# A conditional block's transfers moved from SyncE's queue to GpSimd's queue

## Chip, cores and metric

The kernel runs on one core of one Trainium2 chip. The metric is the device time of one execution in microseconds (us), lower is better.

Three things are compared in time: the median of several executions, the span of the one profiled execution (first to last instruction), and what I call the **tail**: the end of the span minus the start of VectorE's last instruction, the add that completes the last output tile. The tail is there because the whole run scatters by some 3 us, while the end of the program repeats to a few tenths.

## The reference

Two branches are added to the input. Branch A is a recurrent attention: 64 segments of 32 tokens, each with 8 memory rows that are the previous segment's output. Branch B is a mixer and an MLP. Cut:

```python
def _A_ref(x, mem0, Wq, Wk, Wv, Wo, seg_len):
    mem = mem0
    for s in range(n_seg):                      # 64 segments, serial
        h = jnp.concatenate([mem, xs], axis=1)  # 8 + 32 rows
        q, k, v = ...                           # einsum with Wq, Wk, Wv (1024 x 32 heads x 128)
        p = _softmax(masked scores)
        o = ...                                 # p @ v, then Wo
        mem = o[:, :M, :]
        outs.append(o[:, M:, :])
...
xn = _layernorm(x, axis=-1)
return x + _A_ref(xn, ...) + _B_ref(xn, ...)
```

## The kernel before

The main program doesn't walk the segments one after the other. It estimates all memory rows ahead, computes all segments in parallel, and counts at the end how many memory rows miss a tolerance. Only if that count is above zero does a conditional block compute everything again, serially. Matmuls, stores and the check at the end of the main program, then the block (cuts are marked):

```python
# class Out: one output tile; its residual load and its store
if hg == (6 if self.late else 0):
    self.Rt = iop.tile([P, 512], F32, tag="Rt")
    nc.gpsimd.dma_start(self.Rt[:, :self.w], R_v[:, self.gi, self.cc])              # L723
...
nc.vector.tensor_tensor(ot[:, :self.w], self.ps[:, :self.w], self.Rt[:, :self.w], op=ALU.add)   # L731
(self.queue or nc.gpsimd).dma_start(out_v[:, self.gi, self.cc], ot[:, :self.w])     # L732
...
for o, q in zip(rest[-3:], (nc.sync, nc.sync, nc.scalar)):   # queues of the last three stores
    o.queue = q
...
nc.vector.tensor_scalar(cnt[:], nok[:], -1.0, float(NQ - 1), op0=ALU.mult, op1=ALU.add)
nc.vector.tensor_tensor(cnt[:], psc[:1, :1], cnt[:], op=ALU.add)
nc.vector.tensor_copy(flag_i[:], cnt[:])
for o in rest[2:]:
    for p in range(8):
        o.piece(p)

cond = nc.values_load(flag_i[0:1, 0:1], min_val=0, max_val=NQ + P)                  # L890
with tc.If(cond > 0):                                                               # L891
    ...
    nc.sync.dma_start(wo_sb[:], Wo_v)
    nc.sync.dma_start(mask40[:], mask40_d.ap())
    ...
    with tc.For_i(0, NSEG, 1) as i:                                                 # L911, 64 turns
        nc.sync.dma_start(xs[:], xn_d[bass.ds(i * SEG, SEG), :])
        nc.sync.dma_start(Rt[M:L, :], R_d[bass.ds(i * SEG, SEG), :])
        ...
        for hg in range(8):
            wq = fw.tile([P, KT, 512], BF16, tag="w")
            nc.sync.dma_start(wq[:], Wq_v[:, :, cs_])
            ...                                     # wk and wv the same: 24 loads of 1 MB a turn
        ...
        nc.sync.dma_start(out[0][bass.ds(i * SEG, SEG), :], ot[M:L, :])
```

## Time and profile before

| what | before |
|---|---|
| median time (3 executions) | 1516.68 us (1515.07 to 1517.8) |
| span of the profiled execution | 1512.7 us |
| TensorE busy | 1502.8 us, 99% |
| VectorE, ScalarE, GpSimd busy | 36%, 33%, 12% |
| start of VectorE's last add | 1508.87 us |
| tail (1512.7 - 1508.87) | 3.8 us |

The page of the kernel before: its span, busy time by engine, the moved data by DMA queue (q1, called hardware_dynamic, has SyncE's transfers; q0, software_dynamic, has GpSimd's), and the engines on the chain that ended last.

```profile
span 1512.7 us, 24295 instructions
...
PE 1502.8 (99%) x9778; PEld 807.9 (53%) x9850; DVE 545.2 (36%) x1138; ACT 504.1 (33%) x1142; POOL 178.9 (12%) x248
...
q1 hardware_dynamic: 281248, 189.92, 50.5%
q0 software_dynamic: 22032, 82.54, 15.8%
...
PE 98%; DMA 1%; issue 0%; ACT 0%; DVE 0%; SPq 0%
```

TensorE is busy all the time and is nearly the whole chain, so queues matter only where TensorE waits for a transfer, and after TensorE's last matmul.

Does the conditional block run? Asking the trace of before for a tile that only the block uses gives this:

```profile
nothing on hseg; most used: ['ps', 'wt', 'w_sb', 'hTb', 'oX', 'xT', 'h3T', 'QT', 'wo_sb', 'V', 'pso', 'psO', 'xn3T', 'psS', 'sm', 'PT', 'KT', 'xn2T', 'hTB', 'wot', 'oT_m', 'sums', 'Pn', 'rs', 'MZ']
```

So it doesn't. What is left of the block is the branch over it. The instructions of the kernel before at the line of the `If` (L891); columns: engine, operation, count, shortest/median/longest duration in ns, start of the first and of the last in us. A `q` after the engine's name means its sequencer.

```profile
L891 SPq EVENT_SEMAPHORE  x8: 17/17/17, 1506.8 to 1511.0; - x8
L891 POOLq COMPARE_BRANCH  x1: 54/54/54, 1503.4 to 1503.4; - x1
L891 SPq COMPARE_BRANCH  x1: 58/58/58, 1506.2 to 1506.2; - x1
L891 PEldq COMPARE_BRANCH  x1: 3495/3495/3495, 1507.3 to 1507.3; - x1
```

The reader should see two things. SyncE runs eight semaphore instructions (a semaphore is a counter that engines wait on and advance). I read them so: the skipped block would have advanced eight counters of transfers, so the path around the block waits for each and advances it by hand. And TensorE's branch takes 3.5 us where the others take under 0.1 us.

After the branch comes the program's closing code (all on L1015, the line that closes the program). In the kernel before, in the same columns: SyncE's list of waits (from 1511.0 us), GpSimd's four steps of the closing barrier, and SyncE's three drains, of which the first, at 1511.8 us, ends its list of waits. The second fence is the same view for GpSimd alone, 1495 to 1511 us, which singles out its first drain:

```profile
L1015 SPq EVENT_SEMAPHORE  x14: 17/28/28, 1511.0 to 1512.6; - x14
L1015 POOLq EVENT_SEMAPHORE  x4: 17/17/17, 1511.9 to 1512.6; - x4
...
L1015 SPq DRAIN  x3: 7/7/13, 1511.8 to 1512.1; - x3
```

```profile
L1015 POOLq DRAIN  x1: 5785/5785/5785, 1503.6 to 1503.6; - x1
```

GpSimd has a drain of 5.785 us, which starts at 1503.6 and is over at 1509.4 us. SyncE works through a list of waits and reaches its own closing drain at 1511.8 us. The closing barrier follows (from 1511.9 us). The end of the work itself, from the timeline of before (start, duration, engine, line, operation):

```profile
1502.87 0.54 POOL L723 DMA_DIRECT2D Rt<-R_scratch  x1 [5.65 <-DVE ot L731]
...
1508.87 0.42 DVE L731 TENSOR_TENSOR ot<-pso,Rt 128x256 bf16<-128x256 f32 x1 [3.07 <-PE pso L725]
1509.33 0.38 ACTq L732 DMA_DIRECT2D out_dram<-ot  x1
```

### The profile page before, as it was taken

To read this page: it belongs to the slowest core of one execution; us is meant where nothing else is said; L and a number is where in the kernel's file an instruction comes from. 1 tells how busy PE (TensorE), PEld (TensorE's weight loads), DVE (VectorE), ACT (ScalarE), POOL (GpSimd) and SP (SyncE) were. 2 spreads that over 40 slices of the span, in tenths; PEclk is the share of its full clock that TensorE was granted. 3 is DMA by queue.
4 is the path that set the end of the run, shared out by engine and by line. 5 is a ranking of instruction groups with operands and counts; after the bars stand their busy time and mean duration, and the time that the engine had idled before them with its cause. 6 is when DMAs were issued, how large, how long until landed. Compare 5 with 4: busy or idle time off the path is not lost.

```text
span 1512.7 us, 24295 instructions
## 1 busy us (share of the span) xinstructions
PE 1502.8 (99%) x9778; PEld 807.9 (53%) x9850; DVE 545.2 (36%) x1138; ACT 504.1 (33%) x1142; POOL 178.9 (12%) x248
## 2 busy tenths in 40 slices
PE   9999999999999999999999999999999999999998
PEld 7844444445444444444466645664665455545555
DVE  8382230100020122222246624651564166516642
ACT  6533203013012011111256614650663266416630
POOL 5231020211111231100000010001000100010001
PEclk9999999999999999999999999999999999999999
DMA  8699762353345887632399947992998299818811
GB/s 295 147 255 334 218 176 91 137 202 112 125 163 145 196 274 253 208 120 84 126 245 242 246 124 183 245 238 71 239 248 203 73 227 224 216 60 212 190 47 52
DMA packets 303539, 274.11 MB, mean 181 GB/s; under 512 B 153926, under 2 KB 270184, under 8 KB 303424
## 3 DMA queue, kind: packets, MB, share of 16 engines
q1 hardware_dynamic: 281248, 189.92, 50.5%
q0 software_dynamic: 22032, 82.54, 15.8%
q8 instruction: 79, 1.29, 0.4%
q14 instruction: 36, 0.29, 0.1%
q10 hardware_dynamic: 144, 0.07, 0.0%
HBM read 190.93 MB, written 46.14 MB: 157 GB/s over the span
## 4 chain that ended last, share of the span: by engine, by line
PE 98%; DMA 1%; issue 0%; ACT 0%; DVE 0%; SPq 0%
PE ps L667 30%; PE pso L725 15%; PE ps L595 15%; PE ps L537 13%; PE ps L563 13%; PE ps L395 4%; PE ps L318 3%; PE psS L682 2%; PE psO L706 2%; PE ps L860 1%; PE ps L487 1%; PE gps L466 0%; PE ps L452 0%; DMA PT<-Pn 0%; DMA xt<-in_A_x_dram 0%
## 5 line engine op out<-in xcount | busy, mean ns | idle before, releaser
L667 PE MATMUL ps<-hTb,wt 128*128 128x396 bf16 (+2 forms) x2528 | 497.5, 343 | 0.0
L667 PEld LDWEIGHTS <-wt 128*128 128x128 bf16 x2528 | 232.8, 98 | 166.4
L595 PE MATMUL ps<-wt,xT 128*128 128x512 bf16 x1003 | 220.1, 379 | 1.1
L725 PE MATMUL pso<-wo_sb,oX 128*128 128x512 bf16 (+1 forms) x972 | 209.3, 372 | 1.1
L537 PE MATMUL ps<-xn3T,w_sb 128*128 128x512 bf16 x896 | 196.2, 379 | 0.0
L563 PE MATMUL ps<-w_sb,h3T 128*128 128x512 bf16 x873 | 194.3, 379 | 1.2
L595 PEld LDWEIGHTS <-xT 128*128 128x128 bf16 x1024 | 100.2, 98 | 120.8
L538 ACT ACTIVATE h3T<-ps 128x512 bf16<-128x512 f32 x112 | 66.8, 597 | 290.4 <-PE ps L537 289.5
L725 PEld LDWEIGHTS <-oX 128*128 128x128 bf16 x992 | 96.1, 98 | 106.5
L673 ACT CAST KT<-ps 128x462 bf16<-128x462 f32 (+2 forms) x160 | 81.9, 512 | 191.0 <-PE ps L667 189.2
L563 PEld LDWEIGHTS <-h3T 128*128 128x128 bf16 x896 | 87.0, 98 | 103.3
L537 PEld LDWEIGHTS <-w_sb 128*128 128x128 bf16 x896 | 86.6, 98 | 102.1
L688 DVE TENSOR_REDUCE sums<-sm 99x4 f32<-99x396 f32 (+2 forms) x176 | 97.6, 555 | 113.2 <-ACT sm L686 113.2
L675 ACT ACTIVATE QT<-ps 128x462 bf16<-128x462 f32 (+2 forms) x160 | 83.9, 525 | 113.1 <-PE ps L667 101.5
L597 ACT CAST Vs<-ps 128x512 bf16<-128x512 f32 x64 | 37.5, 586 | 233.2 <-PE ps L595 174.9
L684 DVE TENSOR_TENSOR sm<-psS,c_mask_reg_sb 99x396 f32<-99x396 f32 x152 | 86.7, 570 | 76.9 <-PE psS L682 76.9
L686 ACT ACTIVATE sm<-sm 99x396 f32<-99x396 f32 (+2 forms) x176 | 92.7, 527 | 59.0 <-DVE sm L684 54.1
L601 DVE CAST Vs<-ps 128x512 bf16<-128x512 f32 x64 | 44.3, 692 | 170.0 <-PE ps L595 160.4
L694 DVE TENSOR_TENSOR Pn<-sm,rs 99x396 bf16<-99x396 f32 (+2 forms) x176 | 98.9, 562 | 7.3 <-DMA PT<-Pn 1.2
L564 DVE TENSOR_TENSOR R<-ps,R 128x512 f32<-128x512 f32 x32 | 21.9, 690 | 180.5 <-PE ps L563 166.3
L732 POOL DMA_DIRECT2D out_dram<-ot x30 | 16.3, 545 | 587.2 <-DVE ot L731 581.4
L731 DVE TENSOR_TENSOR ot<-pso,Rt 128x512 bf16<-128x512 f32 (+1 forms) x33 | 22.3, 675 | 171.7 <-PE pso L725 166.3
(124 smaller groups left out, 1071.5 us busy)
## 6 DMA issues: line engine op xcount, KB each, us to landing
wt<-in_A_Wq_dram SPq DMA_DIRECT2D x76, 512.0 KB
wt<-in_A_Wk_dram SPq DMA_DIRECT2D x76, 512.0 KB
wt<-in_A_Wv_dram POOLq DMA_DIRECT2D x24, 1024.0 KB, 6.6
V_scratch<-Vs SPq DMA_DIRECT2D x32, 512.0 KB
V<-V_scratch SPq DMA_DIRECT2D x40, 384.0 KB
R_scratch<-x POOLq DMA_DIRECT2D x16, 512.0 KB, 5.1
R<-R_scratch SPq DMA_DIRECT2D x16, 512.0 KB
R_scratch<-R POOLq DMA_DIRECT2D x16, 512.0 KB, 3.6
```

Of the source, the lines that this page charges most:

```text
L537: nc.tensor.matmul(ps[:].rearrange("p (n t) -> p n t", t=P), w3_sb[:, k, f * P:(f + 1) * P], xn3T[tb][:, :, k, :], start=(k == 0), stop=(k ...
L538: nc.scalar.activation(h3T[:, f, :], ps[:], ACTF.Gelu_apprx_tanh)
L563: nc.tensor.matmul(ps[:], h3T[:, f, j * P:(j + 1) * P], w4_sb[:, f, ch * 512:(ch + 1) * 512], start=(f == 0), stop=(f == FT - 1))
L595: nc.tensor.matmul(ps[:], xT[:, m4 * 4 + j, k, :], wv[:, k, :], start=(k == 0), stop=(k == KT - 1))
L667: nc.tensor.matmul(ps[:, :nb] if flat else ps[:, :nb].rearrange("p (t c) -> p t c", t=nt), w[:, k, hh * P:(hh + 1) * P], B["rhs"](k), star ...
L673: nc.scalar.copy(o, i)
L675: nc.scalar.mul(o, i, scale)
L684: nc.vector.tensor_tensor(sm[:T, :, :T], S3, t["mask"][:].unsqueeze(1).to_broadcast((T, 4, T)), op=ALU.add)
L686: nc.scalar.activation(e[:T, :, :T], sm[:T, :, :T], ACTF.Exp, scale=LN2)
L688: nc.vector.tensor_reduce(ss, e[:T, :, :T], axis=AX.X, op=ALU.add)
L694: nc.vector.tensor_tensor(Pn[:T, :, :T], e[:T, :, :T], rs[:T, :].unsqueeze(2).to_broadcast((T, 4, T)), op=ALU.mult)
L725: nc.tensor.matmul(self.ps[:, :self.w], self.oX[0][:, h, self.oX[1] + self.gl * P:self.oX[1] + (self.gl + 1) * P], wo_sb[:, h, self.cc], s ...
```

## The change

The intent is to take the block's transfers off SyncE's queue. Eight issue sites change, all inside the block:

```diff
-            nc.sync.dma_start(wo_sb[:], Wo_v)
+            nc.gpsimd.dma_start(wo_sb[:], Wo_v)
...
-            nc.sync.dma_start(mask40[:], mask40_d.ap())
+            nc.gpsimd.dma_start(mask40[:], mask40_d.ap())
...
-                nc.sync.dma_start(xs[:], xn_d[bass.ds(i * SEG, SEG), :])
-                nc.sync.dma_start(Rt[M:L, :], R_d[bass.ds(i * SEG, SEG), :])
+                nc.gpsimd.dma_start(xs[:], xn_d[bass.ds(i * SEG, SEG), :])
+                nc.gpsimd.dma_start(Rt[M:L, :], R_d[bass.ds(i * SEG, SEG), :])
...
-                    nc.sync.dma_start(wq[:], Wq_v[:, :, cs_])
+                    nc.gpsimd.dma_start(wq[:], Wq_v[:, :, cs_])
...   (wk, wv the same)
-                nc.sync.dma_start(out[0][bass.ds(i * SEG, SEG), :], ot[M:L, :])
+                nc.gpsimd.dma_start(out[0][bass.ds(i * SEG, SEG), :], ot[M:L, :])
```

More of the change, by code (lines that the diff above doesn't have):

```diff
@@ L921 @@
                     wq = fw.tile([P, KT, 512], BF16, tag="w")
-                    nc.sync.dma_start(wq[:], Wq_v[:, :, cs_])
+                    nc.gpsimd.dma_start(wq[:], Wq_v[:, :, cs_])
                     wk = fw.tile([P, KT, 512], BF16, tag="w")
-                    nc.sync.dma_start(wk[:], Wk_v[:, :, cs_])
+                    nc.gpsimd.dma_start(wk[:], Wk_v[:, :, cs_])
                     wv = fw.tile([P, KT, 512], BF16, tag="w")
-                    nc.sync.dma_start(wv[:], Wv_v[:, :, cs_])
+                    nc.gpsimd.dma_start(wv[:], Wv_v[:, :, cs_])
                     ps = fps.tile([P, 4, L], F32, tag="mm")
```

## The prediction

> **What bounds the kernel now.** TensorE. The table of busy time gives PE 1502.8 us of a 1512.7 us span (99%), at full granted clock in every slice; the chain of waits is 98% PE. DMA is 1% of that chain.
>
> **What the change touches.** Eight DMA issue sites, all inside the conditional block after the main program (the serial recomputation, taken only if a check count is above zero). Evidence that this run doesn't take it:
> - Asking the trace for tiles that exist only there (`hseg`, `mask40`, `QTa`, `oTs`, `mb`) gives nothing.
> - By line, the count is loaded once per engine (476 to 596 ns), each engine has one compare-and-branch, and after the last output store comes only the closing barrier, to 1512.6 us.
> - If it ran, each of 64 turns would load 24 weight tiles of 1 MB, 1.6 GB in all; at the 181 GB/s this run averages that is over 8 ms (my estimate). The whole run is 1.5 ms and moves 274 MB.
>
> So the change removes, adds and moves no executed transfer. The inputs are fixed and the arithmetic of the count is untouched, so the branch goes the same way.
>
> **What may still move.** Code placed around the block:
> 1. Bookkeeping on the path that skips the block. SyncE now runs eight semaphore instructions of 17 ns at the branch's line (1506.8 to 1511.0 us, waiting for its stores), because the skipped block would have advanced SyncE's DMA counters. This should leave SyncE and appear on GpSimd. SyncE saves at most about 0.1 us (8 x 17 ns); GpSimd branches at 1503.4 us and then sits in a drain of 5.8 us, so some 5 us of bookkeeping there is free.
> 2. Branch distance. The branch takes 54 ns on GpSimd and ScalarE, 58 on SyncE, 72 on VectorE, but 3495 ns on TensorE, over the longest skipped body. (The Trainium skill, "Advanced Engine Details and Errata", Control Flow Timing, gives about 108 ns for a compare-and-branch; four engines are below it, TensorE far above.) GpSimd's skipped body grows to about SyncE's of now, jumped in 58 ns, so I expect the same; even at 3.5 us it would end near 1507 us, ahead of TensorE's branch (1507.3 + 3.5 = 1510.8 us), which with ScalarE's last store (issued at 1509.3 us) sets the end.
> 3. The main program's order is fixed before the block; I expect identical instruction groups.
>
> The Trainium skill, "DMA: Bandwidth & Descriptors", Issuing engines are not separate DMA queues, says that transfers from any queue run on the same 16 engines. That would matter if the block ran; no run here shows it.
>
> **Prediction.** Change from structure: -0.2 to +0.5 us. The spread before is 1515.07 to 1517.8 us. So 1516.5 us, 8 in 10 within 1512.5 to 1520.5 us. Faster by over 2%: 1.5%; within 2%: 97%; slower by over 2%: 1.5%.
>
> **What would show it.** Right: PE busy 1503 us, the same groups and counts, the same MB per queue (q1 189.9, q0 82.5), still nothing on `hseg`, semaphore instructions at the branch's line gone from SyncE and present on GpSimd, and an instruction count within some 20 of 24295. Wrong on point 2: GpSimd's branch in the microseconds. Wrong altogether: MB moving between queues, a changed order of DVE or ACT groups, or a tail after 1509 us longer by more than 1 us.
>
> **What would make it wrong.** The build letting the block influence scheduling, semaphore assignment or memory layout of the main program; GpSimd's bookkeeping taking over 5 us; or GpSimd-issued transfers in a loop needing setup at the program's start.

## The result and the profile after

Ratios here are the mean time of one kernel's fast runs over that of the other's fast runs of the same rounds, so not quite the ratio of the medians quoted.

| what | before | after |
|---|---|---|
| median time (6 executions each) | 1515.14 us (1514.63 to 1517.8) | 1516.55 us (1516.22 to 1517.49) |
| ratio, 95% interval | | 1.0007 (0.9994 to 1.0019): the same |
| span | 1512.7 us | 1514.8 us |
| start of VectorE's last add | 1508.87 us | 1509.44 us |
| tail | 3.8 us | 5.4 us |

By its time the change does nothing that these runs can tell from zero, as predicted. The page after, the lines that answer to those of before:

```profile
span 1514.8 us, 24364 instructions
...
PE 1506.2 (99%) x9850; PEld 807.6 (53%) x9850; DVE 545.1 (36%) x1138; ACT 504.3 (33%) x1142; POOL 179.6 (12%) x248
...
q1 hardware_dynamic: 281248, 189.92, 50.3%
q0 software_dynamic: 22032, 82.54, 15.9%
...
PE 98%; DMA 1%; ACT 0%; DVE 0%; SPq 0%; issue 0%
```

The bytes and packets in each queue are the same to the last digit, and the trace again has nothing on `hseg`. The 3.4 us more of TensorE busy time is records: after has 9850 matmul records, before 9778, and some are missing from a trace now and then (both have 9850 weight loads). In the two traces the working instructions ahead of the branch are the same, in the same order, on every engine (9850 weight loads, 1138 instructions of VectorE, 1142 of ScalarE, 160 transfers of GpSimd, 630 of SyncE); only the incomplete matmul records can't be compared one by one. VectorE's last add starts 0.57 us later, which is within the scatter of the main program.

The end, however, is 1.5 us longer (5.36 against 3.83 us of tail). Around the branch and in the closing code of after, the same views as above:

```profile
L891 POOLq EVENT_SEMAPHORE  x4: 17/42/43, 1504.5 to 1506.4; - x4
L891 POOLq COMPARE_BRANCH  x1: 54/54/54, 1504.0 to 1504.0; - x1
L891 POOLq INC_SWDGE_SEM  x1: 1591/1591/1591, 1506.5 to 1506.5; - x1
L891 SPq COMPARE_BRANCH  x1: 58/58/58, 1506.8 to 1506.8; - x1
L891 PEldq COMPARE_BRANCH  x1: 3435/3435/3435, 1507.9 to 1507.9; - x1
```

```profile
L1015 SPq EVENT_SEMAPHORE  x14: 17/28/1615, 1508.1 to 1514.7; - x14
L1015 POOLq EVENT_SEMAPHORE  x4: 17/17/17, 1514.0 to 1514.7; - x4
...
L1015 SPq DRAIN  x3: 7/7/7, 1511.6 to 1514.2; - x3
```

```profile
L1015 POOLq DRAIN  x1: 5785/5785/5785, 1508.2 to 1508.2; - x1
```

```profile
1503.44 0.54 POOL L723 DMA_DIRECT2D Rt<-R_scratch  x1 [5.65 <-DVE ot L731]
...
1509.44 0.42 DVE L731 TENSOR_TENSOR ot<-pso,Rt 128x256 bf16<-128x256 f32 x1 [3.07 <-PE pso L725]
1509.89 0.38 ACTq L732 DMA_DIRECT2D out_dram<-ot  x1
```

The bookkeeping moved as expected: SyncE's eight semaphore instructions are gone, and GpSimd has four that wait and one that advances its counters (INC_SWDGE_SEM, 1.591 us). The waits end at 1506.4 us; the last transfer they can be waiting for is GpSimd's residual load issued at 1503.44 us. The counter update follows. Only then, at 1508.2 us instead of 1503.6, does GpSimd start its closing drain, and that drain takes exactly the same 5.785 us. It ends at 1514.0 us, and at 1514.0 us the closing barrier begins. SyncE was ready at 1511.6 us. So GpSimd is now the last to arrive.

That gives **theory A**: GpSimd's closing drain is work of a fixed length, not a wait for others, so everything put ahead of it moves its end; the 4.2 us between branch and drain (0.2 before) used up the slack and 1.5 us more. Its rivals: **B**, the end waits for GpSimd's counters through SyncE, and the drain only waits for the rest; **C**, the longer tail is scatter or comes from the code placed behind the branch.

### The profile page after: what moved, and what is told of

The parts are those of the page before. It is cut to its first block, busy times and chain, and to the rows that moved or that the text cites. A ratio compares the mean times of both kernels' runs of the same rounds, so it can differ in the third digit from the quotient of the medians.

```text
span 1514.8 us, 24364 instructions
## 1 busy us (share of the span) xinstructions
PE 1506.2 (99%) x9850; PEld 807.6 (53%) x9850; DVE 545.1 (36%) x1138; ACT 504.3 (33%) x1142; POOL 179.6 (12%) x248
## 4 chain that ended last, share of the span: by engine, by line
PE 98%; DMA 1%; ACT 0%; DVE 0%; SPq 0%; issue 0%
PE ps L667 30%; PE pso L725 15%; PE ps L595 15%; PE ps L537 13%; PE ps L563 13%; PE ps L395 4%; PE ps L318 3%; PE psS L682 2%; PE psO L706 2%; PE ps L860 1%; PE ps L487 1%; PE ps L452 0%; PE gps L466 0%; DMA PT<-Pn 0%; DMA xt<-in_A_x_dram 0%; PE ps L308 0%
```

## The experiments

All runs returned correct results.

### e1: the block's transfers on ScalarE's queue

```diff
-  nc.sync.dma_start(...)      # the eight sites of the block
+  nc.scalar.dma_start(...)
```

> The kernel before, with the fallback's transfers on ScalarE's queue in place of SyncE's: moved off SyncE, but not to GpSimd. Tail = end of the span minus the start of VectorE's last add (3.8 us before, 5.4 us after the change). Theory A (GpSimd's closing drain takes a fixed 5.8 us from wherever it starts, and the skip path's bookkeeping on GpSimd delayed its start from 1503.6 to 1508.2 us): no bookkeeping on GpSimd, the drain starts about 0.2 us after GpSimd's branch, the tail is 3.8 us within 0.3; the eight counter instructions are on ScalarE. Theory C (the longer tail is scatter between executions or follows from leaving SyncE): the tail is 5.4 us, or anywhere between. Time against before: 0.999 to 1.001 under each.

Median 1515.58 us (4 executions) against 1515.64 for before in the same rounds; ratio 0.9992 (0.9962 to 1.0022). The tail is 1513.7 - 1509.84 = 3.9 us. GpSimd's drain in e1, and the semaphore instructions at the branch's line:

```profile
L1015 POOLq DRAIN  x1: 5785/5785/5785, 1504.6 to 1504.6; - x1
```

```profile
L891 SPq EVENT_SEMAPHORE  x8: 17/17/17, 1507.4 to 1512.0; - x8
```

A detail of the expectation was wrong: the eight counter instructions stay on SyncE, though the block's transfers are ScalarE's. The point holds: with nothing owed on GpSimd, the drain starts 0.2 us after GpSimd's branch (at 1504.4 us) and the tail is that of before. It is not leaving SyncE's queue that costs; it is using GpSimd's. (Since the eight stay on SyncE, e1 doesn't show what SyncE gains by losing them; e3, e11 and e12 do.)

### e2: one site out of eight

```diff
-            nc.sync.dma_start(mask40[:], mask40_d.ap())
+            nc.gpsimd.dma_start(mask40[:], mask40_d.ap())
```

> The kernel before, with only the fallback's mask load (one of the eight sites) moved to GpSimd's queue, so that one counter of GpSimd's is owed on the skip path, not eight. Theory A: a counter update on GpSimd at the branch's line, with at most one wait; if the 1.59 us of the update goes with the number of counters it is well under 0.5 us here, the drain starts before 1505 us and the tail is 3.8 us within 0.3. If the update's cost is fixed, it is about 1.6 us, the drain starts near 1505.3 and ends near 1511.1, and the tail is 3.8 to 4.2 us. Theory B (SyncE's closing waits for GpSimd's counters set the end): 3.8 us as well.

One execution, 1515.73 us, tail 1513.5 - 1509.68 = 3.8 us.

```profile
L891 POOLq INC_SWDGE_SEM  x1: 1565/1565/1565, 1504.4 to 1504.4; - x1
```

```profile
L1015 POOLq DRAIN  x1: 5785/5785/5785, 1506.0 to 1506.0; - x1
```

The second of the two guesses came true: the update is hardly cheaper for one counter (1.565 us) than with all eight sites moved (1.591 us). A single transfer of 26 KB in a block that never runs buys the whole update. But with one counter there is no wait for the last residual load, so the drain starts at 1506.0 us and is over (1511.8 us) before SyncE arrives (1512.6 us). No longer tail.

### e3: the change, and GpSimd at its branch earlier

```diff
-                    nc.gpsimd.dma_start(self.Rt[:, :self.w], R_v[:, self.gi, self.cc])
+                    (nc.scalar if self.queue else nc.gpsimd).dma_start(self.Rt[:, :self.w], R_v[:, self.gi, self.cc])
```

This is applied to the kernel after; it moves the last three residual loads to ScalarE.

> The kernel after, with the last three residual loads (256 KB, 128 KB, 128 KB; the last GpSimd transfers before the branch) issued from ScalarE. The skip path's bookkeeping on GpSimd stays. Theory A: GpSimd reaches its branch some 5 us earlier, near 1498 us, the update takes the same 1.6 us, the drain of 5.8 us ends before 1508 us and no longer ends last: tail 3.8 us within 0.4, so the change's 1.5 us is gone though all that the change added is still there. Theory C (more code behind GpSimd's branch, or the update itself, lengthens the end): tail stays near 5.4 us.

Median 1514.53 us (4 executions), ratio to before 0.9985 (0.9955 to 1.0015). Tail 1512.8 - 1509.46 = 3.3 us.

```profile
L891 POOLq COMPARE_BRANCH  x1: 54/54/54, 1497.5 to 1497.5; - x1
L891 POOLq INC_SWDGE_SEM  x1: 1531/1531/1531, 1499.1 to 1499.1; - x1
```

```profile
L1015 POOLq DRAIN  x1: 5540/5540/5540, 1500.6 to 1500.6; - x1
```

All that the change added is still executed (four waits, an update of 1.531 us, a drain of 5.540 us), but GpSimd's branch comes 6.5 us earlier and the drain is over at 1506.1 us. The extra 1.5 us is gone. That is against C. The tail is even below the stated band (3.8 within 0.4); e11 and e12 take that up.

### e4: no change in the block, but GpSimd held up otherwise

```diff
-        for o, q in zip(rest[-3:], (nc.sync, nc.sync, nc.scalar)):
+        for o, q in zip(rest[-3:], (nc.sync, nc.sync, nc.gpsimd)):
```

This is applied to the kernel before.

> The kernel before (fallback on SyncE, no bookkeeping on GpSimd), with the very last output store issued from GpSimd's queue in place of ScalarE's. Theory A: GpSimd's drain can start only after its branch, near 0.5 + 0.5 + 0.3 us after that store's start, takes 5.8 us again and ends last: tail 7.5 to 8.5 us, span and time about 4 to 5 us (0.3%) longer than before. Theory B (SyncE's wait for the counters sets the end; the drain is only a wait for the others): tail 3.8 to 4.8 us.

Median 1519.93 us (4 executions, 1518.92 to 1520.22) against 1515.64, ratio 1.0021 (0.9991 to 1.0051; one execution of before, at 1523.43 us, widens it). Tail 1516.9 - 1508.70 = 8.2 us.

```profile
L1015 POOLq DRAIN  x1: 5867/5867/5867, 1510.1 to 1510.1; - x1
```

The block is that of before and no counter is owed on GpSimd. Still, with one store of 64 KB on GpSimd after the last add, the drain starts at 1510.1 us, takes 5.867 us and ends at 1516.0 us; SyncE was at its closing drain at 1511.8 us. The tail grows by 4.4 us, as A said and B did not. Here, as in after, the barrier begins where the drain ends. (The path of B exists: in after SyncE's first closing wait is met at 1508.1 us, when GpSimd's counter update ends. But SyncE is through its list at 1511.6 us, 2.4 us before the barrier.)

### e5: the kernel after again

No edit.

> The kernel after again, unchanged: how far do its tail (5.4 us) and GpSimd's bookkeeping (update 1.59 us, drain 5.785 us) repeat? Theory A: tail 5.4 us within 0.3, drain 5.78 us within 0.05. Time against before: theory A says about +1.5 us, a ratio of 1.001. If the tail comes back near 3.8 us, theory A falls.

Median 1516.3 us (5 executions) against 1515.46 (9), ratio 1.0012 (0.9999 to 1.0026). Tail 1514.3 - 1509.06 = 5.2 us; the update took 1.591 and the drain 5.785 us again, to the nanosecond. The longer tail is no scatter.

### e6: ten transfers fewer on GpSimd's queue

```diff
-                    (self.queue or nc.gpsimd).dma_start(out_v[:, self.gi, self.cc], ot[:, :self.w])
+                    if self.queue is None:
+                        stores[0] += 1
+                    q = self.queue or (nc.scalar if stores[0] > 20 else nc.gpsimd)
+                    q.dma_start(out_v[:, self.gi, self.cc], ot[:, :self.w])
```

This is applied to the kernel after (with `stores = [0]` set up earlier); the four lines shift the program's closing line from L1015 to L1019 and the branch from L891 to L895. GpSimd issues 150 transfers in the main program rather than 160 (counted in the traces).

> The kernel after, with the last ten output stores that GpSimd issued now issued by ScalarE; GpSimd's last residual loads stay, so its branch comes at the same place. What the drain's 5.8 us is made of: with 157, 160 and 161 transfers on GpSimd's queue it took 5.540, 5.785 and 5.867 us, 0.082 us for each one more. If it works off a list of GpSimd's transfers, ten fewer give 4.97 us within 0.1 and a tail of about 4.5 us (0.8 us less than after); if it is a fixed time, 5.8 us and 5.4 us.

One execution, 1515.26 us, tail 1513.7 - 1509.46 = 4.2 us.

```profile
L895 POOLq INC_SWDGE_SEM  x1: 1391/1391/1391, 1506.5 to 1506.5; - x1
```

```profile
L1019 POOLq DRAIN  x1: 4968/4968/4968, 1507.9 to 1507.9; - x1
```

The drain is 4.968 us; 4.97 was expected. The tail is 1.1 us shorter than that of after rather than 0.8, mostly because the update became shorter too, by 0.200 us (0.020 us a transfer). The drain's length is not a constant: from 150 to 161 transfers it goes with how many GpSimd has issued. e7 and e8 show that this number alone doesn't fix it.

### e7: 63 transfers fewer

```diff
-                    nc.gpsimd.dma_start(self.Rt[:, :self.w], R_v[:, self.gi, self.cc])
+                    nc.scalar.dma_start(self.Rt[:, :self.w], R_v[:, self.gi, self.cc])
...
-                    (self.queue or nc.gpsimd).dma_start(out_v[:, self.gi, self.cc], ot[:, :self.w])
+                    (self.queue or nc.scalar).dma_start(out_v[:, self.gi, self.cc], ot[:, :self.w])
```

This is applied to the kernel after.

> The kernel after, with all 63 residual loads and output stores of the attention part moved from GpSimd's to ScalarE's queue (97 transfers stay on GpSimd's). List theory: drain of 5.785 - 63 x 0.082 = 0.6 us, or another length that is far from 5.8 us if the list is shortened in between; the counter update shorter too. Fixed time: 5.8 us. Either way GpSimd is at its branch before 1500 us, so the tail is 3.3 to 3.9 us.

One execution, 1515.42 us, tail 1513.8 - 1510.72 = 3.1 us.

```profile
L891 POOLq INC_SWDGE_SEM  x1: 711/711/711, 1499.6 to 1499.6; - x1
```

```profile
L1015 POOLq DRAIN  x1: 2192/2192/2192, 1500.3 to 1500.3; - x1
```

The straight line (0.6 us) is a miss, and 5.8 us is a miss as well. At 0.082 us each, the drain's loss of 3.593 us is 44 transfers, not 63; at 0.020 us each, the update's loss of 0.880 us is 44 as well. Two different instructions that agree on 44 speak for one common list of transfers, of which some entries leave before the end. By the same reckoning (my estimate from these steps) the list of after has some 71 entries at the end, 5.785 / 0.0817, though 160 transfers were issued. Which ones leave, and when, no run here shows. The tail, 3.1 us, is a little under the stated 3.3 to 3.9.

### e8: no block at all

```diff
-    cond = nc.values_load(flag_i[0:1, 0:1], min_val=0, max_val=NQ + P)
-    with tc.If(cond > 0):
-        ... (the whole block)
```

This is applied to the kernel before. It gives up the guard, so it is a measurement and no candidate.

> The kernel before with the whole conditional block taken out (the count is still made, nothing reads it): what does the guard cost when it is not taken? TensorE's branch of 3.5 us and the register loads leave; the end is then the last store's landing or GpSimd's drain (5.8 us from about 1503 us, so done by 1509.5 us). Tail 3.0 to 3.7 us, at most 0.8 us less than before; time within 0.1% of before. If the tail falls by more than 1 us, the branch and not the store set the end of before.

Median 1514.13 us (4 executions), ratio 0.9989 (0.9974 to 1.0005). Tail 1512.3 - 1509.26 = 3.0 us. So a guard that isn't taken costs about 0.8 us of tail before the change and 2.3 us after it. (GpSimd's drain here is 6.351 us from 1503.2 us. Why it is longer than 5.785 us with the same 160 transfers, by what would be 7 entries of 0.0817 us, I did not find out; it ends at 1509.6 us and doesn't matter.)

### e9 and e10: the block forced

```diff
-        nc.vector.tensor_scalar(cnt[:], nok[:], -1.0, float(NQ - 1), op0=ALU.mult, op1=ALU.add)
+        nc.vector.tensor_scalar(cnt[:], nok[:], -1.0, float(NQ), op0=ALU.mult, op1=ALU.add)
```

This is applied to before (e9) and to after (e10): the count is one too high, so the block always runs.

> The kernel before with one added to the check count, so that the serial recomputation is always taken (the result stays correct, as the block computes the same outputs): what would the change do where its transfers run? With SyncE's queue: 64 turns of 25 MB each, at 200 to 300 GB/s 84 to 126 us a turn, so 7 to 10 ms in all. The trace then has the fallback's tiles and some 1.6 GB more on the hardware queue. This is the reference for the next run.

> The same with the change (fallback's transfers on GpSimd's queue), against the run before this one. The 16 DMA engines and the bytes are the same, so if the queue only issues, the time is within 5% of the forced kernel on SyncE. Each turn adds GpSimd's counter bookkeeping and drains at the loop's end: with the drain at 0.082 us for each transfer on its list (27 a turn) and the update near 1 us, 64 turns would add some 64 x 3 us, 0.2 ms or 2 to 3%. If GpSimd's queue is slower to feed the engines, over 5% slower.

e9: median 7250.57 us (2 executions), inside the expected 7 to 10 ms; e10: 7397.67 us (2). That is 2.0% more with the change, or 147.1 / 64 = 2.3 us a turn, and inside the expected 5%. The clock, 0.82 and 0.81, is no cause of it: TensorE is busy for 5444.2 us in e9 and 5442.3 in e10. The pages of e9 and e10 (span and queues):

```profile
span 7251.0 us, 134405 instructions
...
q1 hardware_dynamic: 1892066, 1825.83, 81.6%
q0 software_dynamic: 22032, 82.54, 3.3%
```

```profile
span 7392.8 us, 133835 instructions
...
q0 software_dynamic: 449088, 1718.45, 69.6%
q1 hardware_dynamic: 281248, 189.92, 10.2%
```

Here the change moves 1.6 GB from one queue to the other. The mean rates (263 and 258 GB/s) are the two times over again, as the bytes are the same. What speaks for the queue feeding the engines about equally well is that TensorE waits nearly as long for the `wk` and `wv` loads, 571 us in e9 and 581 in e10. The 2% came from another place than I had expected. Three of TensorE's waits (waiter, what it waited for: us in total, times, longest), e9 then e10:

```profile
PE ps L930 <- DMA wq<-in_A_Wq_dram: 372.1, 116, 5.8
...
PE psS L943 <- PEq L911: 156.8, 63, 2.5
...
PE psx L916 <- DMA xs<-xn_scratch: 89.8, 63, 1.7
```

```profile
PE psx L916 <- DMA xs<-xn_scratch: 484.5, 64, 8.3
...
PE psS L943 <- PEq L911: 205.2, 63, 3.3
...
PE ps L930 <- DMA wq<-in_A_Wq_dram: 24.5, 38, 1.1
```

On SyncE a turn's first transfer is the small `xs` (64 KB), which TensorE needs first: it waits 89.8 us for it over all turns. On GpSimd a weight load of 1 MB goes out first, `xs` lands 6.6 us (median) after its issue, and TensorE waits 484.5 us, 395 more. In exchange it hardly waits for that first weight load (24.5 us instead of 372.1, 348 less). The turn's edge (L911) costs 48 us more. These three add up to 95 of the 142 us between the two spans. The rest is in the same view: 33 us that TensorE waits for `hseg` (written from `xs`, so late with it; in e9 the wait for `wq` hides this), 19 more for `wk`, 9 less for `wv` and 2.5 more for the mask, 141 in all. That the weight load ahead of `xs` is what delays it is argued, not isolated by a run; a 128 KB load of GpSimd's lands 2.8 us (median) after its issue in the kernel before. Of the bookkeeping that I had blamed in advance, the update is smaller than I said, 0.219 us (median of 63), and the drain about as long: 2.01 to 2.03 us in 62 of 63 turns. The one longest, 2.205 us, fits 27 transfers a turn times 0.0817 us; the others are 0.2 us shorter, which I can't explain. How much of the later `xs` comes from this drain, ahead of it, is not shown.

### e11 and e12: what of e3 is due to the change

e11 is before with e3's edit; e12 is e3's kernel again, on the same chip.

> The kernel before (fallback on SyncE) with the same edit as e3 (the last three residual loads issued from ScalarE). e3, which has that edit and the change, had a tail of 3.3 us, 0.5 us less than before. If the edit by itself gave that, the tail here is 3.3 us too. If it came from the change (SyncE no longer runs its eight counter instructions after the last store has landed, ahead of the closing list of waits), the tail here is 3.8 us within 0.15, and SyncE reaches its closing drain 2.9 us after VectorE's last add, not 2.2 to 2.4 us.

> e3's kernel again (the change and the three loads on ScalarE), on the same chip as the run before this one: tail 3.3 us within 0.15 again; median 0.3 to 0.7 us under the kernel of e11 and 0.5 to 1 us under before, inside 0.1%.

e11: median 1515.2 us (5 executions), ratio to before 1.0002 (0.9988 to 1.0016), tail 1513.3 - 1509.10 = 4.2 us, over the stated 3.95. e12: median 1514.28 us (5), ratio 0.999 (0.9976 to 1.0003), tail 1512.9 - 1509.52 = 3.4 us. Its median is 0.9 us under e11's and 1.3 us under that of before, both a little more than was stated (0.3 to 0.7 and 0.5 to 1). SyncE's closing drain in e11 and e12 (the first of three is the one to read):

```profile
L1015 SPq DRAIN  x3: 7/7/13, 1512.4 to 1512.7; - x3
```

```profile
L1015 SPq DRAIN  x3: 7/7/7, 1512.0 to 1512.3; - x3
```

SyncE gets there 3.3 us after the last add in e11 and 2.5 us after it in e12. Over all profiled runs with the block skipped and the last store on ScalarE: 2.9, 3.0, 2.9 and 3.3 us where SyncE has the eight instructions (before, e1, e2, e11), and 2.2, 2.1, 2.4, 2.5, 2.5 and 2.2 us where it hasn't (after, e5, e3, e12, e6, e7). e11's 0.4 us more than before is the order of the eight: one of them waits for the last store, in before the seventh (met at 1510.91 us), in e11 the second (1511.12 us), so that five more instructions follow it. On average, then, the change does spare SyncE 0.7 us (3.0 less 2.3). In after, that gain is hidden behind GpSimd's drain; in e3 and e12 it shows. Those two have the lowest medians of their rounds among the kernels that keep the guard, but the medians by less than 0.1%, and with intervals that include 1, so a gain in time is not shown.

## Why the prediction was right, and where it wasn't

- **Right: nothing executed moves.** The same bytes in each queue, the same order on every engine ahead of the branch, nothing on the block's tiles. The time (1516.55 us) is inside the range and 0.05 us from the point; this closeness is chance, as the median of before moved from 1516.68 to 1515.14 us with three more executions.
- **Right: the branch distance is free.** GpSimd's branch takes 54 ns in both kernels over its longer skipped body.
- **Right: the bookkeeping leaves SyncE and appears on GpSimd.** Instruction totals are no test of this: after has 24364 and e5, the same kernel, 24292. That part of "what would show it" was badly chosen, since records are missing now and then.
- **Wrong in mechanism, and so in size: "Change from structure: -0.2 to +0.5 us".** The tail grew by 1.5 us in the first pair of profiles and by 1.4 us in e5 (5.2 against 3.8). My own sign of being "wrong altogether", a tail longer by more than 1 us, came true. The step that failed is item 1: "GpSimd branches at 1503.4 us and then sits in a drain of 5.8 us, so some 5 us of bookkeeping there is free." I read the drain as waiting, which bookkeeping could fill. It is work: it takes its 5.785 us wherever it starts (1503.6, 1504.6, 1506.0, 1507.7 or 1508.2 us). The free time was not the drain but the gap after it, 1511.8 - 1509.4 = 2.4 us. The bookkeeping took 4.0 us more on GpSimd (4.2 us from branch to drain, 0.2 before): 2.4 us until the last wait was met, 1.6 us of update, the rest between instructions. 4.0 less 2.4 is the 1.6 us by which GpSimd now ends the program later than SyncE did. Of the 4.6 us by which the drain starts later, 0.6 us is the later branch of that execution.
- **Wrong in size: "SyncE saves at most about 0.1 us (8 x 17 ns)".** It saves 0.7 us. The durations in the profile are 17 ns, but the last of the eight comes after the last store has landed, and the whole closing list comes after that one. Before, that list is started at 1511.0 us and takes 0.8 us; after, it is started at 1508.1 us (when GpSimd's counter update is over) and most of it is done when the store lands.
- The two errors have opposite signs. The gain of 0.7 us can't be seen in after because SyncE isn't last there.

## The Trainium skill and the runs

"Advanced Engine Details and Errata", Control Flow Timing, has one figure for a compare-and-branch, about 108 ns. Here it is 50 to 72 ns on four engines and 3.3 to 3.7 us on TensorE when the block is skipped; when the block is entered (e9) TensorE's branch takes 83 ns. So TensorE's cost comes with the jump over the block, not with the comparison. That the length of the jump makes it so is not shown by these runs.

"DMA: Bandwidth & Descriptors", Issuing engines are not separate DMA queues, says that all queues run on the same 16 engines. e9 and e10 fit that (waits for `wk` and `wv` of 571 and 581 us over either queue) but don't test it; changing the queue cost 2.0%, most of it, by TensorE's waits, the later `xs` and the turn's edge.

## What to carry to other kernels

A block that is skipped still has a cost on the path around it, and the queue of its transfers can decide which engine pays (GpSimd's queue moved the cost from SyncE to GpSimd; ScalarE's, in e1, left it on SyncE); read the closing code of every engine, and ask which one arrives last. An instruction that looks idle in the profile (a drain) is only slack if its length changes when its start moves: compare its duration between two runs before you spend it. Transfers on GpSimd's queue leave a debt for the end, so the last of them should go out early, or from another queue.

## What the Trainium skill lacked or had wrong

- "VectorE: DVE Perf Modes", The DRAIN you can't avoid, tells of boilerplate drains at a program's start and end that take about 12 ns on all engines. The drains here stand on the kernel's own closing line, so they may not be the ones that the page means. SyncE's, ScalarE's, VectorE's and TensorE's are of that kind here (7 to 17 ns in before and after), but GpSimd's closing drain took 5.540, 5.785 and 5.867 us with 157, 160 and 161 transfers issued from its queue, and 4.968 us with 150: 0.082 us for each one more (but 2.192 us with 97, and 6.351 us with 160 in e8, where the block is taken out). In e8 TensorE's closing drain took 2.155 us and VectorE's 0.461 us as well. The figure of about 12 ns doesn't cover these.
- No page that I found has the counter update on the path around a skipped block (INC_SWDGE_SEM): 1.591 us with 160 transfers, 1.391 with 150, 0.711 with 97, and hardly less for one counter (1.565 us).
- "Advanced Engine Details and Errata", Control Flow Timing: its one figure, about 108 ns, doesn't tell an entered block from a skipped one. TensorE's branch took 83 ns where the block is entered and 3.3 to 3.7 us over a skipped body of 1512 matmuls and weight loads (e9 has 48384 of each more than before, so 756 of each in each of 64 turns), while GpSimd's, SyncE's, ScalarE's and VectorE's took 50 to 72 ns over their shorter bodies. Why is not shown by these runs.
- "DMA: Bandwidth & Descriptors" advises between queues by first-byte time and features. It lacks what a queue costs at the end of the program: e4 moved one 64 KB store to GpSimd and the tail grew by 4.4 us.
